# Softmax over the heads of q: the maximum taken off by eight exponentials with a bias, in place of one subtraction on GpSimd

## The chip, the cores and the metric

The kernel runs on one core of a Trainium2 chip. The core has five engines that run their own instruction streams and wait for one another by semaphores: TensorE (PE in the profile, with its weight loads shown apart as PEld), VectorE (DVE), ScalarE (ACT), GpSimd (POOL) and SyncE (SP), which here only starts transfers. The metric is the time of one execution on the device in microseconds (us). Lower is better.

## The reference

Everything is float32. First a linear attention with two softmaxes, then a Fourier mixing layer with a two-layer perceptron:

```
# q, k, v: (batch 8, heads 8, sequence 576, head width 64)
q_s = exp(q - max(q, axis=-1));  q_s = q_s / (sum(q_s, axis=-1) + 1e-9)   # over the 64 of one head
k_s = exp(k - max(k, axis=2));   k_s = k_s / (sum(k_s, axis=2) + 1e-9)    # over the sequence
kv  = einsum('bhsd,bhse->bhde', k_s, v)
x   = einsum('bhsd,bhde->bhse', q_s, kv)          # then laid out as (8, 576, 512)
u   = x + real(fft(fft(x, axis=1), axis=2))
un  = (u - mean(u)) / sqrt(var(u) + 1e-6)
out = u + relu(un @ w_ch1) @ w_ch2                # 512 -> 2048 -> 512
```

The change touches the first line alone: each row of q holds 8 heads of 64 values, and each head has a maximum of its own.

## The kernel before, in words

The eight batch elements are worked through one after the other. For each there is an attention, a Fourier transform with its mixing, a normalisation, and the perceptron. The perceptron does almost all of the multiplying. For the first group of rows it is done plainly (L780 up, L789 down). All later groups use a Strassen scheme (L850 up, L886 down) with seven products in place of eight. Its products gather in the PSUM banks `ba`, `bb`, `bc`; L814 (ScalarE) and L818, L822, L861 (VectorE) take sums of them out, L857 and L862 (ScalarE) are the relus, and L341 to L344 (`a_side`, GpSimd) form the Strassen combinations of the result.

While TensorE does the perceptron of one batch element, the attention of the next one is laid between its steps (`merged`, L1039, L1040). So one stage of the trace, some 122 us long, has an "up" half, in which the attention of the next element runs, and a "down" half, in which its transform, mixing and normalisation run.

The attention of a batch element is a list of items, pipelined over load, exponential, turn (transpose) and product:

- four `k` items (a pair of heads each): `k_exp` takes the maximum (L455), the exponential with the maximum as its bias and the sum as its second output (L457), then `k_turn` (L467, L468, L474, L476) and `k_times_v` (L484, L487);
- four `q` items of 128 tokens by 512 columns (8 heads of 64): `q_exp`, then `q_turn` (four transposes on TensorE, L532; a copy on ScalarE, L539) and `q_times_kv` (L564, copy L566);
- for every second batch element a `t` item, 128 tokens that two elements share: the same `q_exp`, then `t_turn` (L532, L545) and `t_fold`.

That gives 8 x 4 + 4 = 36 runs of `q_exp`. Before the change one run is: maximum over each head on VectorE (L519); subtraction of the eight maxima, spread over 64 columns each, on GpSimd (L520); one exponential over all 512 columns on ScalarE (L521); sum over each head (L523), plus epsilon (L524), reciprocal (L525), product with the reciprocals (L526), all on VectorE. The tiles of q have three buffers (`bufs=3`), the maxima and reciprocals three each.

The order of the instructions on each engine is not written out by hand. The build puts the instructions of each engine into an order of its own from their dependencies and their place in the source, and inserts the waits. In the trace the first exponentials of q for the batch element after the next one stand, for that reason, at the end of an "up" half, ahead of work that comes earlier in the source (L577). Within an engine the order is then fixed: an instruction that waits holds up all behind it.

For the first batch element there is no perceptron to hide behind: its attention, transform and normalisation fill the first 62 us alone, with small matmuls (L206) laid in only to keep TensorE running. Its q lies in the large tile `big`, and one q of the second element lies in `spare`; the other 30 are named `q` in the profile.

## Time and profile before

| | |
|---|---|
| time, median of 3 runs | 1157.17 us (1155.72 to 1157.97) |
| span of the profiled execution | 1153.2 us |
| PE busy | 1102.6 us (96%) |
| DVE busy | 543.1 us (47%) |
| POOL busy | 371.8 us (32%) |
| ACT busy | 352.1 us (31%) |
| mean granted TensorE clock | 0.993 |

Busy time is the sum of the time in which an engine had an instruction in hand. TensorE is busy nearly throughout, so the other engines matter only where TensorE has to wait for them, or where they do before it has begun. The groups of the profile say how often a line ran, how long one took, how long its engine had been idle just before, and what ended that idle time.

The lines of `q_exp` in the trace before: L519 ran 36 times at some 0.68 us, L520 36 times at 1.04 us where nothing else pressed (up to 1.49 us), L521 36 times at 0.63 us, L523 36 times at 0.68 us.

### The profile page before, as it was taken

How to read it: one execution, taken by the hardware profiler on the slowest of the kernel's cores; microseconds unless marked ns; L12 is line 12 of the kernel's file. 1: busy time of each engine (PE TensorE's matmuls, PEld its weight loads, DVE VectorE, ACT ScalarE, POOL GpSimd, SP SyncE). 2: the span in 40 equal slices, each digit the busy share in tenths (PEclk: the TensorE clock that was granted, in tenths of full speed). 3: DMA queues.
4: the chain of work that ended last, by engine and by line, in shares of the span. 5: the costliest groups of instructions: out<-in, count | busy, mean ns of one | idle time of the engine just before them, and what ended most of it. 6: DMA issues, size and time to landing. Idle time of an engine off the chain costs nothing.

```text
span 1153.2 us, 14431 instructions
## 1 busy us (share of the span) xinstructions
PE 1102.6 (96%) x5472; PEld 919.8 (80%) x5472; DVE 543.1 (47%) x1110; ACT 352.1 (31%) x704; POOL 371.8 (32%) x338
## 2 busy tenths in 40 slices
PE   5799989998999999999999999999999999999997
PEld 4644555877888988888889888888889888888886
DVE  6775757368333734376334733583434353202301
ACT  4585422343123412252215222341233142201200
POOL 4075632246103521254023601361033303402320
PEclk9999989999999999999999999999999999999999
DMA  9378765354346534554366334643454344444441
GB/s 313 111 229 267 253 234 191 126 176 158 129 142 202 205 110 150 185 181 147 124 201 212 135 119 149 202 178 137 142 181 153 113 144 167 167 153 153 149 182 55
DMA packets 92548, 193.78 MB, mean 168 GB/s; under 512 B 23088, under 2 KB 59696, under 8 KB 85312
## 3 DMA queue, kind: packets, MB, share of 16 engines
q1 hardware_dynamic: 90680, 191.82, 48.8%
q10 hardware_dynamic: 1800, 1.05, 0.3%
q8 instruction: 43, 0.70, 0.2%
q14 instruction: 25, 0.20, 0.1%
HBM read 168.72 MB, written 28.31 MB: 171 GB/s over the span
## 4 chain that ended last, share of the span: by engine, by line
PE 67%; DVE 7%; ACT 1%; DMA 1%; issue 0%; POOL 0%; POOLq 0%; SPq 0%
PE bb L886 13%; PE bb L850 12%; PE bc L886 10%; PE bc L850 8%; PE ba L850 7%; PE ba L886 7%; PE acc L484 2%; PE acc L564 1%; PE acc L655 1%; PE acc L658 1%; PE tr L750 1%; PE acc L678 1%; DVE eo L603 1%; PE tr L467 1%; PE tr L532 1%; DVE big L861 1%
## 5 line engine op out<-in xcount | busy, mean ns | idle before, releaser
L850 PE MATMUL bb<-unT,big 128*128 128x256 f32 x768 | 187.7, 381 | 2.9 <-DVE u L822 2.8
L886 PE MATMUL bb<-big 128*128 128x256 f32 x768 | 172.8, 379 | 0.0
L850 PEld LDWEIGHTS bb<-unT,big 128*128 128x128 f32 x768 | 142.8, 190 | 26.8 <-DVE u L818 4.1
L886 PEld LDWEIGHTS bb<-big 128*128 128x128 f32 x768 | 145.1, 190 | 20.1
L850 PE MATMUL bc<-unT,big 128*128 128x256 f32 x512 | 125.2, 379 | 0.0
L850 PE MATMUL ba<-unT,big 128*128 128x256 f32 x512 | 124.5, 379 | 0.0
L341 POOL TENSOR_TENSOR big<-big 128x512 f32<-128x512 f32 (+1 forms) x38 | 45.0, 1183 | 246.5 <-ACT big L862 242.0
L886 PE MATMUL bc<-big 128*128 128x256 f32 x512 | 116.5, 379 | 0.5 <-DVE x L903 0.5
L862 ACT ACTIVATE big<-big 128x512 f32<-128x512 f32 x96 | 60.3, 629 | 179.8 <-DVE big L861 179.6
L886 PE MATMUL ba<-big 128*128 128x256 f32 x512 | 114.1, 379 | 0.0
L886 PEld LDWEIGHTS bc<-big 128*128 128x128 f32 x512 | 95.9, 190 | 14.1 <-DVE x L903 0.9
L886 PEld LDWEIGHTS ba<-big 128*128 128x128 f32 x512 | 95.9, 190 | 12.3
L850 PEld LDWEIGHTS bc<-unT,big 128*128 128x128 f32 x512 | 95.5, 190 | 12.5
L850 PEld LDWEIGHTS ba<-unT,big 128*128 128x128 f32 x512 | 95.0, 190 | 11.7
L822 DVE TENSOR_TENSOR u<-bb,s 128x512 f32<-128x512 f32 x40 | 27.6, 690 | 135.7 <-PE bb L886 80.0
L349 POOL TENSOR_TENSOR unT<-unT 128x512 f32<-128x512 f32 x8 | 14.2, 1776 | 174.3 <-DVE unT L348 174.3
L818 DVE TENSOR_TENSOR u<-bb,s 128x512 f32<-128x512 f32 x40 | 27.6, 691 | 82.5 <-PE bb L850 41.7
L898 POOL TENSOR_TENSOR x<-x,u 128x512 f32<-128x512 f32 x14 | 17.8, 1269 | 147.3 <-DVE u L822 118.8
L861 DVE TENSOR_TENSOR big<-bc,u 128x512 f32<-128x512 f32 x64 | 44.0, 688 | 23.1 <-PE bc L850 22.2
L520 POOL TENSOR_TENSOR q<-q,qm 128x512 f32<-128x512 f32 x30 | 32.5, 1089 | 58.1 <-DVE qm L519 22.6
L814 ACT COPY s<-ba 128x512 f32<-128x512 f32 x40 | 23.4, 586 | 91.0 <-PE ba L886 47.5
L342 POOL TENSOR_TENSOR big<-big 128x512 f32<-128x512 f32 (+1 forms) x38 | 47.7, 1254 | 2.0
(224 smaller groups left out, 1652.2 us busy)
## 6 DMA issues: line engine op xcount, KB each, us to landing
big<-w1s SPq DMA_DIRECT2D x64, 896.0 KB
big<-w2s SPq DMA_DIRECT2D x56, 1024.0 KB
big<-in_w_dram SPq DMA_DIRECT2D x21, 512.0 KB
k<-in_kT_dram SPq DMA_DIRECT2D x26, 288.0 KB
q<-in_q_dram SPq DMA_DIRECT2D x27, 256.0 KB
v<-in_v_dram SPq DMA_DIRECT2D x26, 256.0 KB
words<-in_w_dram SPq DMA_DIRECT2D x11, 512.0 KB
w2s<-big SPq DMA_DIRECT2D x8, 512.0 KB
```

The lines of the kernel that those rows point to most:

```text
L341: e1.tensor_tensor(out=to(4), in0=at(2), in1=at(3), op=ALU.add)
L342: e1.tensor_tensor(out=to(2), in0=at(0), in1=at(2), op=ALU.subtract)
L484: nc.tensor.matmul(pk, lhsT=ks[:, c, :], rhs=v[:, c, :], start=(c == 0), stop=(c == NC - 1))
L520: nc.gpsimd.tensor_tensor(out=heads, in0=heads, in1=spread(m), op=ALU.subtract)
L814: nc.scalar.copy(temp("s1"), box["ba"][:])
L818: V.tensor_tensor(out=temp("u2"), in0=box["bb"][:], in1=box["s1"][:], op=ALU.add)
L822: V.tensor_tensor(out=temp("u3"), in0=box["bb"][:], in1=box["s1"][:], op=ALU.add)
L850: nc.tensor.matmul(bank()[:, i, :], lhsT=w[:, WA_AT[m], k * P:(k + 1) * P], rhs=unT[:, B_AT[m], k, :], start=first and i == 0 and k == 0, ...
L861: V.tensor_tensor(out=hp(i), in0=bank[:], in1=u[:], op=ALU.add)
L862: nc.scalar.activation(hp(i), hp(i), ACT.Relu)
L886: nc.tensor.matmul(bank()[:, i, :], lhsT=h[p][:, A_AT[m], i * P:(i + 1) * P], rhs=w[:, p, :], start=first and i == 0 and p == 0, stop=p == ...
L898: nc.gpsimd.tensor_tensor(out=x, in0=x, in1=t[:], op=ALU.add)
```

## The change

The subtraction on GpSimd is left out. The maximum is written with its sign turned, and ScalarE takes it off as the bias of the exponential. A bias is one value per partition, and a row has eight heads with eight maxima, so the one exponential over 512 columns becomes eight over 64 columns. What is computed stays the same. The change takes a step and a hand-over between engines out of the chain, and takes work off GpSimd; ScalarE gets more instructions.

```diff
         m = self.small.tile([P, H], F32, tag="qm", name="qm", bufs=3)
-        V.reduce_max(m[:], heads, axis=AX.X)
-        nc.gpsimd.tensor_tensor(out=heads, in0=heads, in1=spread(m), op=ALU.subtract)
-        nc.scalar.activation(q, q, ACT.Exp)
+        V.reduce_max(m[:], heads, axis=AX.X, negate=True)
+        for h in range(H):
+            nc.scalar.activation(heads[:, h, :], heads[:, h, :], ACT.Exp, bias=m[:, h:h + 1])
         rec = self.small.tile([P, H], F32, tag="qrec", name="qrec", bufs=3)
         V.reduce_sum(rec[:], heads, axis=AX.X)
```

## The prediction

> **What bounds the kernel now.** I read the busy times first, then the granted clock, then who waited for whom on TensorE, then the order of time around the lines that change.

> ```profile
> span 1153.2 us, 14431 instructions
> PE 1102.6 (96%) x5472; PEld 919.8 (80%) x5472; DVE 543.1 (47%) x1110; ACT 352.1 (31%) x704; POOL 371.8 (32%) x338
> L520 POOL TENSOR_TENSOR q<-q,qm 128x512 f32<-128x512 f32 x30 | 32.5, 1089 | 58.1 <-DVE qm L519 22.6
> ```

> TensorE is the bound: it is idle for only 1153.2 - 1102.6 = 50.6 us, of which 62.0 - 38.65 = 23.3 us lie in the first 62 us, where the first batch element is prepared alone (busy times by stretches). Nothing taken off GpSimd or put on ScalarE counts by itself. What counts is what it does to those waits. The list of waits of TensorE names few that touch `q_exp`:

> ```profile
> PE bb L850 <- DVE u L822: 2.8, 1, 2.8
> PE acc L564 <- ACT qT L539: 2.4, 4, 1.7
> PE tr L532 <- DVE big L526: 1.5, 2, 1.0
> PE tr L532 <- DVE q L526: 0.7, 2, 0.4
> PE tr L532 <- DVE qrec L524: 0.5, 1, 0.5
> PE tr L532 <- ACT q L521: 0.3, 1, 0.3
> ```

> (us in all, times, longest.) The largest, 2.8 us, seems to have nothing to do with q. The order of time shows that it has:

> ```profile
> 262.72 0.66 DVE L519 TENSOR_REDUCE qm<-q 128x8 f32<-128x512 f32 x1
> 265.82 1.27 POOL L344 TENSOR_TENSOR big<-big 128x512 f32<-128x512 f32 x1
> 267.05 1.04 POOL L520 TENSOR_TENSOR q<-q,qm 128x512 f32<-128x512 f32 x1
> 268.12 0.63 ACT L521 ACTIVATE q<-q 128x512 f32<-128x512 f32 x1 [4.56 <-POOL q L520]
> 268.79 0.69 DVE L523 TENSOR_REDUCE qrec<-q 128x8 f32<-128x512 f32 x1 [3.33 <-ACT q L521]
> 271.75 0.68 DVE L822 TENSOR_TENSOR u<-bb,s 128x512 f32<-128x512 f32 x1
> 272.48 1.13 PE L850 MATMUL bb<-unT,big 128*128 128x256 f32 x4 [2.85 <-DVE u L822]
> ```

> The maximum was ready at 263.38, but the subtraction stood behind L341 to L344 on GpSimd until 267.05. ScalarE waited for it, VectorE's sum L523 for ScalarE, L822 stood behind that on VectorE, and TensorE waited for L822. So GpSimd's queue did cost TensorE 2.85 us, once. In the later stages (530 us on) TensorE never waits at L532: the exponential is there early.

> [...] L457 (bias, 576 columns) takes 772 ns and L730 (bias, 4 columns) 297 ns, so some 293 fixed with a bias. Four L744, which have two such operands (806 ns each), ran in 2.93 us from 443.76 on: (2.93 - 0.81)/3 = 0.71 us apart, an overlap of 0.10 us.
> [...] L520 took 1.04 us alone, but 1.37 us at 254.60, beside L526 and L861. [...] what negating a maximum costs; L455 does it already, in some 0.75 us for 576 columns, against 0.68 for the 512 of L519, so I cost it at nothing.

> **The change, part by part.**
> Removed: 36 subtractions of 1.04 us, some 37 us of GpSimd, and one hand-over. Nobody waits for the freed GpSimd directly.
> Added: seven more instructions on ScalarE for each of 36 runs. [...] one after another 346 - 96 = 250 ns. Eight: 7 x 0.25 + 0.35 = 2.10 us. No row shows short instructions with a bias in a row. Bounds: L666 follows L664 after only 0.09 us (32 columns, no bias), which would give some 1.1 us; no overlap at all gives 8 x 0.346 = 2.77 us. I take 2.10, since L744 shows the overlap with such operands.
> A lone run of `q_exp`, from the end of the maximum to the end of the exponential. Before: 0.13 (L519 to L520, at 503.05) + 1.04 + 0.03 + 0.63 = 1.83 us. After: 0.04 (L455 to L457, at 491.71) + 2.10 = 2.14 us. So 0.31 us later. ScalarE itself stood still for most of the 1.83 before (it waited for q on GpSimd 25 times, 35.1 us in all), so what stands behind it on ScalarE is late by the same 0.31 us. But where two runs follow each other, GpSimd and ScalarE worked side by side before, one every 1.04 us; now it is one every 2.0 us, so the second is late by 0.31 + 0.96 = 1.27 us. In all ScalarE gets 36 x (2.0 - 0.53) = 53 us more to do, which 31% busy carries.

> What of it reaches TensorE, stretch by stretch, with the order as it is:
> - First element (0 to 62 us, nothing hides anything). Two runs at 15.24 and 15.96 follow each other: the second ends 0.9 us later than 19.15. Behind it on ScalarE stand L545 and L468, and TensorE waits for both already (L474 and L484, at 19.68 and 20.16). The last run (26.26; its subtraction took 1.29 us) loses 0.1 to 0.3. Sum: +1.1.
> - Second element (137 to 163 us). Three runs in a row: 24 short exponentials take 6.1 us, and end at 144.4 in place of 142.9. L468 behind them has 1.25 us to spare; the fourth run gets later on VectorE, and L539 behind it, for which L564 already waits 1.7 us. Sum: +0.8.
> - Third element (240 to 275 us). TensorE waits 0.3 to 0.5 us at four L532, so there is no slack. The first two runs follow each other and VectorE does the second sum ahead of the first product: +1.2; the third adds 0.3. Then the wait at 272.48: the exponential no longer stands behind L344, but all has moved by 1.5 us. Following the same queue, maximum end 264.9, eight exponentials to 267.1, L523 to L526 to 269.0, two L519 to 270.2, L822 to 270.9: TensorE goes on at 270.9 in place of 272.48. Sum of the stretch: -1.6.
> - Stages for elements five and seven (from 498 and 744 us). L539 stands behind two runs on ScalarE and TensorE waits for it already by 0.2 and 0.4 us (507.17, 752.79): each +0.7.
> - Ends of the other "up" halves (388 to 398, 633 to 644 us). Two runs follow each other, VectorE falls back by 0.4 us, and the transform's chain there ends in a TensorE wait of 1.2 us (L655, at 411.73 and 657.17): each +0.4.
> - All other runs: the product L526 ends 2.8 us (505.33 against L532 at 508.17) to 100 us before its transpose. TensorE's L850 hides them.
> Sum: 1.1 + 0.8 - 1.6 + 1.4 + 0.8 = +2.5 us. 1157.2 + 2.5 = 1159.7 us.

> The build orders the instructions anew, since the change gives it other instructions. It can put L545 or L539 between short exponentials, or move transposes. I can't read that from the profile; it is the largest unknown, and I put 3 us on it each way.

> **The rivals.**
> Faster: the queue on GpSimd is what TensorE feels. It costs 2.85 us once and holds ScalarE up 25 times (at most 4.6 us). If the new order hides the longer trains at 16 and 245 us (no +1.1, no +1.5), what stays is the whole 2.85 us and some of the small L532 waits (1.5 us in all): 1157.2 - 4 = 1153 us. Against it: the pairs stand there because their data arrive together.
> No difference: the longer trains lie beside L850 and L886 everywhere but in the first 62 us, and the losses there are paid by the wait at 272. For it: no wait at L532 from 530 us on. 1157 us.
> Much slower: short exponentials with a bias overlap less than L744, 0.35 us each, 2.8 us a run. A run is then 1.0 us later and each of a pair 2.0. The eight or so runs without slack lose some 0.7 us more each, 5.6 us: 1159.7 + 5.6 = 1165 us. Against it: the row of L744.

> **How the numbers follow.** The forecast of 1159.7 has a chance of 0.36, the much slower case 0.11, no difference 0.27, faster 0.26. The bounds of 0.2% are 1154.9 and 1159.5. Slower is the forecast and the much slower case, 0.47; same 0.27; faster 0.26. The range takes in the faster rival and the much slower one, with 2 us more on each side for the order: 1151 to 1167 us.

> **What would show it right or wrong.** L520 is gone and L521 is there 288 times with some 0.35 us each, 0.25 us apart; ACT busy rises by some 36 x (8 x 0.35 - 0.63) = 78 us in the profile's way of counting, POOL falls by 38. The wait of L850 for L822 at 272 us shrinks; the waits of L474, L484 and L532 before 62 us and around 250 us grow. If trains are much longer or shorter than 2.1 us, my price is wrong. If TensorE's idle time of the first 62 us falls, or the waits at 250 us do, the new order has done better than I could read, and the time is below the one before.

## The result, and the profile after

| | before | after |
|---|---|---|
| time, median of 4 runs | 1156.68 us (1155.72 to 1157.97) | 1142.61 us (1140.6 to 1143.67) |
| ratio, 95% interval | | 0.9876 [0.9858, 0.9894] |
| span of the profiled execution | 1153.2 us | 1140.2 us |
| TensorE busy, and not busy | 1102.6, 50.6 us | 1098.6, 41.6 us |

The changed kernel is 14.1 us faster; 1159.7 was predicted, and the time lies below the range. The first lines of the page after, and the group of the new exponentials:

```profile
span 1140.2 us, 14639 instructions
PE 1098.6 (96%) x5472; PEld 919.1 (81%) x5472; DVE 543.4 (48%) x1110; ACT 397.7 (35%) x956; POOL 332.5 (29%) x302
L521 ACT ACTIVATE q<-q,qm 128x64 f32<-128x64 f32 x240 | 61.5, 337 | 10.2 <-DVE qm L519 9.4
```

GpSimd lost 39.3 us of work and ScalarE got 45.6 us more, as the change means it to. The 13.0 us of span are TensorE's: 9.0 us less in which it has nothing in hand, and 4.0 us less for the same 5472 matmuls. The list of TensorE's waits after, the rows of L655, L532, L474, L850 and L564 that answer to those of before (us in all, times, longest):

```profile
PE tr L532 <- DVE q L526: 2.2, 3, 1.3
PE acc L655 <- DVE eo L625: 0.7, 2, 0.6
PE tr L474 <- ACT tq L545: 0.3, 1, 0.3
PE bb L850 <- DVE u L822: 0.3, 1, 0.3
PE acc L564 <- ACT qT L539: 0.2, 1, 0.2
```

Before, these lines had 2.8 for L822, 2.4 for L539, 2.9 for L625, 0.9 for L545, and 3.0 for the four rows of L532 (big, q and qrec from VectorE, q from ScalarE). Four of the five were to grow by the prediction; all four fell, L532 the least (in the third element it did grow, from 1.4 to 2.2).

Where the time went. The first L780, the first L789, and the first L850 or L886 of a stage are the same products in both traces, so the difference of their starts is what had been gained by then (one execution of each kernel; two further profiles of the changed kernel stand beside it below):

| stretch before | what runs beside it | predicted | trace |
|---|---|---|---|
| 0 to 62.6 us | first element alone | +1.1 | -1.6 |
| 62.6 to 120.2 | k of the second element | 0 | -1.4 |
| 120.2 to 208.2 | q of the second element, weights of the Strassen scheme | +0.8 | -4.7 |
| 208.2 to 278.7 | "up" half with the third element | -1.6 | -2.6 |
| 278.7 to the end | the other stages | +2.2 | -2.9 |
| sum | | +2.5 | -13.1 |

**The third element.** All engines after, in the order of time, around the place where L822 stood behind the exponential (rows between are left out):

```profile
255.27 1.27 POOL L344 TENSOR_TENSOR big<-big 128x512 f32<-128x512 f32 x1
257.93 1.26 DVE L519 TENSOR_REDUCE qm<-q 128x8 f32<-128x512 f32 x2
258.83 3.69 ACT L521 ACTIVATE q<-q,qm 128x64 f32<-128x64 f32 x15
261.57 0.68 DVE L822 TENSOR_TENSOR u<-bb,s 128x512 f32<-128x512 f32 x1
262.16 0.68 DVE L523 TENSOR_REDUCE qrec<-q 128x8 f32<-128x512 f32 x1
262.41 1.03 PE L850 MATMUL bb<-unT,big 128*128 128x256 f32 x4
```

ScalarE begins 0.9 us after the first of two maxima has begun; L344 plays no part. L822 now stands ahead of the sum L523 on VectorE, and the L850 behind it starts without a wait.

**The first element.** ScalarE after, where the prediction had the second of two runs 0.9 us late, and with it L545 and L468:

```profile
16.05 2.26 ACT L521 ACTIVATE big<-big,qm 128x64 f32<-128x64 f32 x9 [0.25 <-DVE qm L519]
18.21 0.56 ACT L545 COPY tq<-tr 128x512 f32<-128x512 f32 x1
18.68 0.58 ACT L468 COPY ks<-tr 128x512 f32<-128x512 f32 x1
19.15 2.02 ACT L521 ACTIVATE big<-big,qm 128x64 f32<-128x64 f32 x8
```

The build laid the two copies between the short exponentials (after nine of them), so that they did not wait for the second train. L545, which began at 19.05 before, begins at 18.21, and TensorE's L484 behind them at 19.31 in place of 20.16. The other half of the 1.6 us comes by 31 us: the later runs of q end earlier too, and the two waits of L532 for L526, 1.03 and 0.45 us before, are gone.

**The second element.** ScalarE and TensorE before, at the first product of q with kv:

```profile
148.60 0.63 ACT L521 ACTIVATE spare<-spare 128x512 f32<-128x512 f32 x1 [4.81 <-POOL spare L520]
149.26 0.59 ACT L539 COPY qT<-tr 128x512 f32<-128x512 f32 x1
149.90 0.94 PE L564 MATMUL acc<-kvr,qT 128*128 128x128 f32 x6 [1.70 <-ACT qT L539]
152.26 0.79 PE L564 MATMUL acc<-kvr,qT 128*128 128x128 f32 x2 [1.43 <-DVE kvr L487]
153.70 3.62 PE L789 MATMUL ba<-big 128*128 128x512 f32 x4
```

Both after, at the same place:

```profile
142.33 2.00 ACT L521 ACTIVATE spare<-spare,qm 128x64 f32<-128x64 f32 x8
144.36 0.58 ACT L539 COPY qT<-tr 128x512 f32<-128x512 f32 x1
145.29 0.83 PE L564 MATMUL acc<-kvr,qT 128*128 128x128 f32 x6
147.60 0.49 PE L564 MATMUL acc<-kvr,qT 128*128 128x128 f32 x2 [1.48 <-DVE kvr L487]
148.36 1.88 PE L789 MATMUL ba<-big 128*128 128x512 f32 x4
```

Of two waits one is left, and the four L789 behind them take 1.88 us in place of 3.62: the granted clock was 0.57 on the mean from 151 to 159 us before, and 1.00 in the same window after. The starts of the same products give each its share. Before the first L564 the changed kernel is 2.7 us ahead, at its last product (147.60 against 152.26) 4.7, and at the first L789 behind the halved clock (151.41 against 159.02) 7.6. So the wait brings some 1.9 us of this stretch and the clock some 2.9.

The wait is gone because of the order. On ScalarE, L539 stands behind the exponential of `spare`, whose maximum (L519, VectorE) began at 146.68 before, 9.1 us after the start of the three maxima ahead of it; the build now puts it at 138.73, 3.9 us after their start. The subtraction of `spare` on GpSimd began only 0.17 us after its maximum had ended, so GpSimd's queue held it for almost nothing.

**An "up" half further on.** Rows of GpSimd before, at the end of the stage of the third element, whose "down" half begins at 398.30 before and at 388.16 after:

```profile
394.12 1.37 POOL L520 TENSOR_TENSOR q<-q,qm 128x512 f32<-128x512 f32 x1 [3.25 <-DVE qm L519]
395.45 1.72 POOL L603 TENSOR_TENSOR eo<-x 128x512 f32<-128x512 f32 x1
400.00 1.45 POOL L603 TENSOR_TENSOR eo<-x 128x512 f32<-128x512 f32 x1
```

GpSimd after, at the same place:

```profile
377.96 1.27 POOL L603 TENSOR_TENSOR eo<-x 128x512 f32<-128x512 f32 x1
383.89 1.38 POOL L603 TENSOR_TENSOR eo<-x 128x512 f32<-128x512 f32 x1 [4.67 <-ACT x L566]
```

L603 is the first step of the transform. Its two runs stood behind the subtractions of q for the element after the next, 2.9 us ahead of the "down" half and 1.7 us into it. Without them the build has it 10.2 and 4.3 us ahead. Its chain ended in the wait of L655 for L625 at 411.73, 1.17 us; after, that L655 starts at 400.25 without one. The same happened at 657.17 (1.16 us). It is L603's place that counts, and not the empty queue as such: in a run below that gives GpSimd its old amount of work back, L603 comes 5.0 and 3.7 us ahead of the "down" half, and the wait is gone as well.

### The profile page after: what moved, and what is told of

Its sections match the earlier page's. It is cut to its first block, busy times and chain, and to the rows that moved or that the text cites. A ratio compares the mean times of both kernels' runs of the same rounds, so it can differ in the third digit from the quotient of the medians.

```text
span 1140.2 us, 14639 instructions
## 1 busy us (share of the span) xinstructions
PE 1098.6 (96%) x5472; PEld 919.1 (81%) x5472; DVE 543.4 (48%) x1110; ACT 397.7 (35%) x956; POOL 332.5 (29%) x302
## 4 chain that ended last, share of the span: by engine, by line
PE 79%; DVE 11%; ACT 4%; DMA 2%; issue 2%; POOL 1%; SPq 0%; ACTq 0%; POOLq 0%; DVEq 0%
PE bb L850 14%; PE bb L886 13%; PE bc L886 10%; PE bc L850 9%; PE ba L850 9%; PE ba L886 8%; PE acc L484 3%; PE acc L564 2%; PE bc L789 2%; PE acc L655 2%; PE acc L658 2%; PE acc L678 1%; PE tr L750 1%; PE tr L532 1%; PE tr L467 1%
## 5 line engine op out<-in xcount | busy, mean ns | idle before, releaser
L850 PE MATMUL bb<-unT,big 128*128 128x256 f32 x768 | 187.9, 381 | 0.3 <-DVE u L822 0.3
L886 PE MATMUL bb<-big 128*128 128x256 f32 x768 | 172.8, 379 | 0.0
L850 PEld LDWEIGHTS bb<-unT,big 128*128 128x128 f32 x768 | 142.8, 190 | 23.8 <-DVE u L818 3.4
L886 PEld LDWEIGHTS bb<-big 128*128 128x128 f32 x768 | 145.1, 190 | 20.1
L341 POOL TENSOR_TENSOR big<-big 128x512 f32<-128x512 f32 (+1 forms) x38 | 45.1, 1187 | 309.5 <-ACT big L862 305.6
L850 PE MATMUL bc<-unT,big 128*128 128x256 f32 x512 | 125.3, 379 | 0.0
L850 PE MATMUL ba<-unT,big 128*128 128x256 f32 x512 | 124.3, 379 | 0.0
L886 PE MATMUL bc<-big 128*128 128x256 f32 x512 | 116.5, 379 | 0.5 <-DVE x L903 0.5
L886 PE MATMUL ba<-big 128*128 128x256 f32 x512 | 114.1, 379 | 0.0
L886 PEld LDWEIGHTS bc<-big 128*128 128x128 f32 x512 | 95.9, 190 | 14.1 <-DVE x L903 0.9
L886 PEld LDWEIGHTS ba<-big 128*128 128x128 f32 x512 | 95.9, 190 | 12.3
L850 PEld LDWEIGHTS bc<-unT,big 128*128 128x128 f32 x512 | 95.5, 190 | 12.5
L850 PEld LDWEIGHTS ba<-unT,big 128*128 128x128 f32 x512 | 95.0, 190 | 11.7
L822 DVE TENSOR_TENSOR u<-bb,s 128x512 f32<-128x512 f32 x40 | 27.6, 689 | 134.8 <-PE bb L886 79.1
L521 ACT ACTIVATE q<-q,qm 128x64 f32<-128x64 f32 x240 | 61.5, 337 | 10.2 <-DVE qm L519 9.4
L349 POOL TENSOR_TENSOR unT<-unT 128x512 f32<-128x512 f32 x8 | 14.2, 1773 | 172.9 <-DVE unT L348 172.9
L818 DVE TENSOR_TENSOR u<-bb,s 128x512 f32<-128x512 f32 x40 | 27.6, 690 | 76.8 <-PE bb L850 38.1
L861 DVE TENSOR_TENSOR big<-bc,u 128x512 f32<-128x512 f32 x64 | 44.1, 688 | 26.1 <-PE bc L850 25.3
L754 ACT COPY unT<-tr 128x512 f32<-128x512 f32 x36 | 20.6, 585 | 86.5 <-PE tr L750 86.0
```

The lines of the kernel that those rows point to most:

```text
L341: e1.tensor_tensor(out=to(4), in0=at(2), in1=at(3), op=ALU.add)
L521: nc.scalar.activation(heads[:, h, :], heads[:, h, :], ACT.Exp, bias=m[:, h:h + 1])
L818: V.tensor_tensor(out=temp("u2"), in0=box["bb"][:], in1=box["s1"][:], op=ALU.add)
L822: V.tensor_tensor(out=temp("u3"), in0=box["bb"][:], in1=box["s1"][:], op=ALU.add)
L850: nc.tensor.matmul(bank()[:, i, :], lhsT=w[:, WA_AT[m], k * P:(k + 1) * P], rhs=unT[:, B_AT[m], k, :], start=first and i == 0 and k == 0, ...
L861: V.tensor_tensor(out=hp(i), in0=bank[:], in1=u[:], op=ALU.add)
```

## The experiments

The theory formed from this: **the gain is GpSimd's queue**, of which the subtractions are gone, so that everything behind them on GpSimd, and what follows that on the other engines, comes earlier. Rivals: **the short pieces**, between which the build can lay copies; **ScalarE's and VectorE's shorter chain**, whatever GpSimd does; **the clock**, of which a lucky position of the waits gives or takes a stretch. The short diffs are against the kernel before, where nothing else is said.

### Which part brings it

VectorE subtracts, one exponential, nothing of q on GpSimd:

```diff
-        nc.gpsimd.tensor_tensor(out=heads, in0=heads, in1=spread(m), op=ALU.subtract)
+        V.tensor_tensor(out=heads, in0=heads, in1=spread(m), op=ALU.subtract)
```

> The subtraction goes to VectorE (36 more instructions of some 0.68 us there), the exponential stays one of 512 columns. Theory A (the gain of 14 us comes from taking q out of GpSimd's queue: q stood behind L341 to L344 there, and L603 and L341 stood behind q): most of the gain is here too, 1141 to 1149 us. Theory B (the gain comes from the short exponentials, between which the build can put copies that TensorE waits for): none of it is here, 1154 to 1162 us.

Measured: 1150.52 us, 0.9964 [0.9951, 0.9976]. A part of the gain only, between the two ranges of the expectation. VectorE pays 36 x 0.68 = 24 us for what GpSimd lost. By the first L206 the trace is 1.2 us later than before (the change is 1.6 earlier), TensorE waits 3.1 us for L818 in place of nothing, and L655 waits 3.1 us as before. So with VectorE loaded for it, freeing GpSimd brings about a third of the gain.

The subtraction stays on GpSimd, eight exponentials without a bias:

```diff
-        nc.scalar.activation(q, q, ACT.Exp)
+        for h in range(H):
+            nc.scalar.activation(heads[:, h, :], heads[:, h, :], ACT.Exp)
```

> The subtraction stays on GpSimd, and the exponential is eight of 64 columns without a bias. Theory A: no gain, and the longer trains on ScalarE come on top of the wait for GpSimd, 1156 to 1164 us. Theory B: most of the gain, 1142 to 1149 us.

Measured: 1152.62 us, 0.9971 [0.9959, 0.9983]. It lies in neither range. The first 62 us are 2.1 us longer, the way that the prediction expected of the trains, but in sum the pieces alone bring 0.29%; that the order which they get repays more than they cost is the likely reading, and not shown.

One maximum for the whole row (the 8 heads share it), one exponential with it as the bias, nothing on GpSimd:

```diff
-        V.reduce_max(m[:], heads, axis=AX.X)
-        nc.gpsimd.tensor_tensor(out=heads, in0=heads, in1=spread(m), op=ALU.subtract)
-        nc.scalar.activation(q, q, ACT.Exp)
+        V.reduce_max(m[:, 0:1], q, axis=AX.X, negate=True)
+        nc.scalar.activation(q, q, ACT.Exp, bias=m[:, 0:1])
```

> One maximum over the whole row of 512 columns as the bias of one exponential, in place of one for each head: nothing on GpSimd and no train of short instructions. The softmax over each head stays the same but for rounding, as its maximum cancels; for widely different heads it would be less safe. If the trains of 2.02 us on ScalarE still cost TensorE something (L532 waits 2.2 us for the third element), some 1 to 3 us below the changed kernel. If they are hidden, the same as the changed kernel. Theory B (short pieces help): some us above the changed kernel.

Measured: 1143.57 us, 0.9897 [0.9858, 0.9936], beside 1143.11, 0.9893 [0.9865, 0.992] for the change itself on the same chip (its expectation stands next). One piece of some 0.72 us does as well as eight in 2.02 us. So the short pieces aren't needed for the gain, and in sum they cost nothing here: what both kernels share is that GpSimd has left the chain and VectorE got nothing. The two don't gain in the same places: this one gains 4.5 us in the stretch of the third element, where the changed kernel gains 2.6, and less before it.

> The changed kernel once more, for a second trace and a ratio beside the other runs on the same chip. If the halved clock comes with the waits, its trace has no halved clock between 125 and 165 us again; if it comes by chance, it may have one there and be some 3 us longer. Ratio to before 0.987 to 0.991.

The changed kernel with two useless subtractions on GpSimd behind each maximum (5 x 64 and 3 x 64 columns, the result is not read), so that GpSimd has its old work back while the chain of q doesn't pass through it:

```diff
+        junk = self.work.tile([P, 5, DH], F32, tag="junk", name="junk", bufs=1)
+        for n in (5, 3):
+            wide = m[:, 0:n].unsqueeze(2).to_broadcast([P, n, DH])
+            nc.gpsimd.tensor_tensor(out=junk[:, 0:n, :], in0=wide, in1=wide, op=ALU.subtract)
```

> The changed kernel, with two instructions of 5 and 3 x 64 columns on GpSimd after each maximum, whose output nobody reads (they stand for the time of the subtraction, not for its place in the chain of q). If it is only q's wait in the queue that cost time, the changed kernel's 1143 us stay, within 2 us. If GpSimd's time as such cost it (what stands behind q on GpSimd, and its press on VectorE), part of the gain goes: 1146 to 1154 us. Theory B: no change from 1143 us.

Measured: 1147.84 us, 0.9936 [0.992, 0.9953]. Some 5 to 7 us of the gain are gone (5 by the medians against the changed kernel's, 7 by the ratios). In the trace all of the loss falls in the first three elements (at the first L886, 278.7 us before, only 2.9 us of gain are left, against 10.2); from there to the end it gains 2.4 us, nearly as the change does. In the second element the dummies stand in front of L349 and L341, and TensorE's product waits longer than before the change:

```profile
151.65 0.79 PE L568 MATMUL acc<-kvr,qT 128*128 128x128 f32 x2 [3.88 <-DVE kvr L487]
153.08 3.62 PE L793 MATMUL ba<-big 128*128 128x512 f32 x4
```

(L568 and L793 are L564 and L789; four lines were put in.) So the load on GpSimd costs in the first two elements, and the later ones gain without it being gone. Whether it costs by delaying what stands behind it on GpSimd, by slowing VectorE's operations beside it (last section), or by the order that this kernel got, this run doesn't tell.

### Where it is

The form of after in the first branch, that of before in the second: for the first three elements alone, and for the last five alone (`it[1] >= 3`):

```diff
+        if it[1] < 3:
...
+        else:
...
```

> The changed form for the first three batch elements, the old one for the other five. The marks of the two traces put 10.2 us of 13.1 before the third element's attention ends. Theory A or B with the gain where the traces show it: 1145 to 1149 us. If the later stages with their shorter queues held most of it: 1151 us or more.

> The counterpart of the run with the first three: the changed form for the last five batch elements alone. In the traces the changed kernel gains 2.95 us after the third element's attention, and the run with the first three gained nothing there. If the gain lies where the traces show it, and the stages don't depend on one another: some 3 us below the kernel before, 1151.5 to 1154. If the stages before set the later ones up: no gain.

Measured: 1146.43, 0.9923 [0.9909, 0.9938], and 1148.31, 0.9934 [0.991, 0.9957]. Together these are 0.77% + 0.66% = 1.43%, more than the 1.07% to 1.24% of the whole change in three comparisons: parts don't add up, since each variant gets an order of its own. The second brought more than the expectation had. One cause shows in its trace: the tile behind L344 in the stage of the third element belongs to the element after it, so that "the last five" holds the longest wait, which falls from 2.85 to 1.07 us. Another 3.3 us of its trace lie before 208 us, where its q is that of the kernel before; they are order and clock. The two parts do agree on the ends of the two "up" halves: with the last five changed each gains 1.4 us, with the first three 0.0.

That one tile alone:

```diff
+        if it == ("q", 3, 0, 0):
...
+        else:
...
```

> The changed form for one q tile of 36: the fourth element's first, whose subtraction stood behind L341 to L344 on GpSimd at 263 to 267 us, before TensorE's wait of 2.85 us for L822. If the prediction read that chain right: that wait goes to under 1 us, and the kernel is 2 to 3 us below the one before. If another subtraction or wait takes its place: under 1 us.

Measured: 1151.7 us, 0.9966 [0.9956, 0.9977]; the stretch of the third element is 2.6 us shorter in its trace. Rows of it in the order of time (L522 is the line of the exponentials in this form; with five lines more, L827 and L855 are L822 and L850):

```profile
263.15 2.01 ACT L522 ACTIVATE q<-q,qm 128x64 f32<-128x64 f32 x8
268.88 0.68 DVE L827 TENSOR_TENSOR u<-bb,s 128x512 f32<-128x512 f32 x1
269.62 1.13 PE L855 MATMUL bb<-unT,big 128*128 128x256 f32 x4 [0.29 <-DVE u L827]
```

One run in 36 brings a quarter of the gain, and the wait that the prediction read in the profile, GpSimd's L344 to TensorE, was read rightly: 2.85 us to 0.29.

The one run of `spare` in the second element, which stood on GpSimd ahead of the second wait there:

```diff
+        if it == ("q", 1, 1, 1):
...
+        else:
...
```

> The changed form for one q tile of 36, the one in the spare tile of the second batch element. In the trace before, TensorE waits 1.70 us for L539 behind it, and its clock is at half from 151 to 158 us. If that clock follows from the waits: the wait and some 3 us of clock go, 3 to 5 us below the kernel before. If the clock falls by itself: 1.7 us below at most. If the wait only moves to the next one behind it (L487 for the second product): nothing.

Measured: 1154.31 us, 0.9991 [0.9979, 1.0003]. No difference that can be told. The waits were 1.86 and 0.79 us in place of 1.70 and 1.43, and a halved clock stayed, for 3.41 us in place of 6.83. The maximum of `spare` began at 145.86, 9.1 us after the start of the three maxima ahead of it, as in the kernel before. The second element's gain is not in that one tile, since its place on VectorE didn't move.

### The second element: the clock, or a chain that ends later

The biggest part of the gain, 4.7 us in the profile, has two readings. (In two further profiles of the changed kernel it was 3.1 and 2.7 us; both had a stretch of 3.41 us at half clock from 127 or 128 us on, behind L484.) The two waits of 1.70 and 1.43 us let the clock be halved, and without the first it isn't; or a chain of the other engines ends earlier. To tell them apart, the waits are filled with other work: products of a unit matrix with itself into the same place, ahead of the first and the last product of the first tile, which the real product then overwrites.

```diff
         for r in range(NR):
-            nc.tensor.matmul(px[:, r * P:(r + 1) * P], lhsT=qT[:, r, :], rhs=self.kvr[b % 2][:, r, :], start=True,
-                             stop=True)
+            at = px[:, r * P:(r + 1) * P]
+            for _ in range(12 if it[1:] == (1, 0, 0) and r in (0, NR - 1) else 0):
+                nc.tensor.matmul(at, lhsT=self.ident[:], rhs=self.ident[:], start=True, stop=True)
+            nc.tensor.matmul(at, lhsT=qT[:, r, :], rhs=self.kvr[b % 2][:, r, :], start=True, stop=True)
```

In the kernel before:

> The kernel before, with 24 small matmuls of the unit matrix (128 x 128, some 0.1 us each) laid on TensorE into the two waits of the second element's first product (1.70 us for L539 and 1.43 us for L487 at 148 to 152 us); the product overwrites what they give. They take no time that TensorE doesn't wait anyway. If TensorE's clock falls to half at 151 to 158 us because it has been waiting: no halved clock there, and up to 3 us below the kernel before. If the clock falls whatever TensorE does: the same as the kernel before, or 0.5 us longer.

In the changed kernel, with 24 more ahead of k's first product in that element:

> The same filling on the changed kernel, and 24 small matmuls more ahead of the second element's first product of k with v, where TensorE waits 2.7 to 3.3 us (L484, at 126 us) and the second trace of the changed kernel has a halved clock. If the clock follows from the waits: no halved clock from 120 to 165 us, and 0 to 2 us below the changed kernel (ratio to before 0.986 to 0.989). If not: the changed kernel's time.

Measured: 1165.83 us, 1.0085 [1.007, 1.0099], and 1152.66 us, 0.9974 [0.9964, 0.9984]. Both miss, since the filling was too much: each product shows as two in the trace, and twelve took 2.84 us, more than the wait. In the first there was no halved clock at 150 us, but new waits of 3.33 and 4.44 us at the transform, each with a halved clock behind it; in the second the filling took 5.5 + 2.8 + 2.8 us, which alone is about what it lost against the change, and a halved clock came at 140 us with a new wait of 3.22 us. Neither decides.

Six in place of twelve, in the kernel before (the expectation's "a quarter of an hour's worth less" is a slip for half of the filling of the first):

> The kernel before with 6 + 6 matmuls of the unit matrix in the second element's first product (12 + 12 passes of 0.11 us, some 1.35 us in each of the waits of 1.70 and 1.43 us), a quarter of an hour's worth less than the run before it: the work now fits into the waits. If the clock falls because TensorE waits there: no halved clock from 145 to 165 us in its trace, and 1 to 3 us below the kernel before. If not: the same as the kernel before.

Measured: 1155.69 us, 1.0 [0.999, 1.001]. The filling fits: six take 1.50 us, 0.34 us of the waits are left, and there is no halved clock up to 165 us. That half of the expectation came true: with the waits filled the halved clock goes, and TensorE is ready for the transform's first L655 at 178.2 us, 2.9 us ahead of 181.06 in the kernel before. The gain of time did not come, since TensorE then waits there (L657 and L627 are L655 and L625):

```profile
182.09 0.73 PE L657 MATMUL acc<-ft,eo 128*128 128x144 f32 x4 [3.92 <-DVE eo L627]
```

The chain of waits that ends there, in pieces (start us, us, what; lines up to L392 are those of before):

```profile
139.92 1.23 POOL q L520
145.65 0.68 DVE q L526
146.34 0.33 DVE big L344
149.90 3.87 DMA w1s<-big
154.63 10.40 DMA w2s<-big
165.12 0.44 DVE big L348
167.50 2.98 DMA w2s<-big
170.50 0.43 DVE big L348
```

It runs from GpSimd's subtraction through ScalarE and VectorE to L344, which here forms combinations of the weights (the same helper as on GpSimd) and stands behind the sums and products of q on VectorE. A store (`w1s`) takes these to memory. On SyncE a load that needs it (L392) stands next, and behind that load the stores of other combinations (`w2s`), 10.40 us for the first. L348 overwrites what that store reads, and the transform follows on VectorE.

This chain is not what held the kernel before. There the second L625, which L655 waits for, had ended 2.9 us before L655 began:

```profile
177.87 0.48 DVE L625 TENSOR_TENSOR eo<-eo 128x128 f32<-128x128 f32 x2
181.06 0.66 PE L655 MATMUL acc<-ft,eo 128*128 128x144 f32 x4
```

(the row holds two runs, of which the first ended at 178.16). In the filled kernel it ended at 181.95. Its build put a maximum of k and a third L348, which waits for a second store of 2.98 us, ahead of VectorE's L603: that starts at 173.13 there and at 167.22 before. So the filling took away the clock's loss, and an order of its own gave it back.

In the changed kernel the same chain comes early. VectorE before, at the L348 behind the first store:

```profile
164.70 0.43 DVE L348 TENSOR_TENSOR big<-big 128x256 f32<-128x256 f32 x1 [11.43 <-DMA w2s<-big]
```

VectorE after:

```profile
158.25 0.43 DVE L348 TENSOR_TENSOR big<-big 128x256 f32<-128x256 f32 x1 [9.74 <-DMA w2s<-big]
```

It comes 6.4 us earlier, of which 3.0 had been gained by 120 us, and L625 ends at 171.97, 1.5 us before L655 at 173.45. Had it gained only those 3.0 us, L655 would have waited some 1.7 us (an estimate: 178.16 - 3.0 against 173.45). So the earlier chain was needed for a part of the 4.7 us.

### A version beyond both

Since TensorE still waits three times (2.2 us) at L532 in the third element, that element's exponential was made in one piece again, behind a subtraction on VectorE; the others as changed (a diff against the changed kernel, which ran beside it):

```diff
+        if it[1] == 2:
+            V.reduce_max(m[:], heads, axis=AX.X)
+            V.tensor_tensor(out=heads, in0=heads, in1=spread(m), op=ALU.subtract)
+            nc.scalar.activation(q, q, ACT.Exp)
+        else:
...
```

> The changed form, but for the third batch element the subtraction on VectorE and one exponential of 512 columns (as in the run with the subtraction on VectorE, which gained 4.0 us in that stretch, where the changed kernel gained 2.6 and waits 2.2 us at L532). If the trains on ScalarE cost that, those waits go and it is 1 to 2 us below the changed kernel. If VectorE's 0.68 us a run cost as much: the same.

> The changed kernel beside the run with VectorE for the third element, on the same chip. Ratio to before 0.987 to 0.991.

Measured: 1141.94 us, 0.9874 [0.9861, 0.9887], and 1142.27, 0.9878 [0.9864, 0.9891]: no difference. The waits of L532 for L526 are gone, but others came in their place: 0.7 us for L857, 1.1 in two for L539, 0.3 each for L818 and L822 (by the names of after). No version was found that is faster than the change.

## Why the prediction was wrong

**Right.** The price of the train: 2.10 us worked out, 2.02 measured, pieces of 337 ns on the mean (346 worked out) that follow each other by 0.24 us. The rows of the trace before give its terms: L457 and L730, both with a bias, took 772 ns for 576 columns and 297 for 4, which is 0.83 ns a column and some 294 for the rest, so some 347 for 64 columns (an estimate from these two); and the four L744 of 806 ns in 2.93 us overlap by 0.10 us each. GpSimd's work, 38 to fall and 39.3 fallen. ScalarE's rise, 78 in the profile's way of counting, was 45.6, since overlapping pieces count once (240 of 337 ns make 80.9 us, and the page has 61.5); nothing in the time hung on that. The third element: L344's hold on TensorE, -1.6 net, was -2.6, and the run with that one tile shows the wait go. The sign that it gave for a time below the one before, less idle time in the first 62 us, came true.

**Wrong, and it is what decided: "Nobody waits for the freed GpSimd directly", and with it the whole list worked out "with the order as it is".** The order was no disturbance of 3 us each way around a sum; it was most of the effect. Four terms failed by it:

- First element, +1.1 predicted, -1.6 in the trace. The pair of trains did not stand as a block in front of L545 and L468; the build laid these between, and the last runs of q, which were to lose 0.1 to 0.3 us, no longer held L532.
- Second element, +0.8 predicted, -4.7, -3.1 and -2.7 in three profiles. The prediction had L539 later, behind longer trains; it came 4.9 us earlier, 2.2 of these gained here, since the build moved the maximum of `spare` ahead. Nor did it look at the granted clock around the waits that it named: of the 4.7 us the wait of 1.70 us makes some 1.9, and the halved clock behind it some 2.9. It also stopped at L564 and did not ask what stood behind q on VectorE, the chain through the stores, which had to come earlier too.
- Ends of two "up" halves, +0.8 predicted, and with the waits of 1.17 and 1.16 us gone, -1.4 each. The prediction had seen those waits, and the subtractions in front of L603 on the same page, but put L655's wait down to VectorE, where the releaser's name stands, and not to the place of L603 on GpSimd ahead of it.
- Elements five and seven, +1.4 predicted; their waits for L539 are gone too.

The remaining -1.4 us, between 62 and 120 us, is a stretch of halved clock which in the kernel before lay on the L780 products (5.4 us for what takes 3.6), and in the changed one on the small L206 that only keep TensorE running. That place is in part chance: of the six traces whose first two elements, but for `spare` or the filling, are those of the kernel before, three have a halved clock at the first L780 and three have not; of the three of the changed kernel none has.

The rival "faster" named GpSimd's queue, which is the mechanism in the third element, but counted only its one visible wait and some waits of L532: 4 us. More of the size would have come from asking, at each of TensorE's waits, what stood in front of the whole chain and not only in front of the engine that released it, and from reading the clock behind it.

**What stays open.** GpSimd's queue itself is shown as the cause in the third element alone, by the run with one tile (2.6 us in its trace, 0.34% of the time). The share of the clock in the whole can only be estimated: its mean was 0.991 over 91 runs of the kernel before and 0.996 over 12 of the changed one, which over 1150 us is some 5 us of the 13 or 14, or three stretches of 3.41 us at half rate. Why the build moves the maximum of `spare`, L603 and L545 as it does was not varied. How much of the whole is the free GpSimd, and how much is an order that happens to suit: a part of the change can't be made with the order of all else held fast, and the experiments that held back some of it (0.9964, 0.9971, 0.9936, 0.9923, 0.9934) don't add up. That the maximum over the whole row, with another set of instructions, gives the same time speaks for GpSimd's place in the chain and against luck, but it is one case, and it gains in other places.

## What to carry to other kernels

When an operation leaves an engine with an in-order queue, follow what stood behind it there, and behind its followers on their engines, through to stores and reused buffers, up to the engine that sets the end; a wait need not be due to the engine that the list names last. A forecast "with the order as it is" says little where a build reorders everything: an engine at 32% of busy time can hold up the one at 96% at places that don't show its name. Behind each wait look at the granted clock, and ask for the next limit before calling a wait free: where one is filled, another can end last.

## What was not expected of the hardware

**The halved clock, behind waits of 2.15 us and more, and in a grid.** In the sixteen traces, after the first 70 us, every wait of TensorE of 3.2 us or more (ten of them, 3.22 to 4.44 us) was followed by a stretch at half clock. So were six of 2.15 to 2.98 us, while ten others of 2.18 to 2.94 us were not (the 2.85 us up to 272.48 before is one of them); and the 1.70 + 1.43 us within 4.4 us in the kernel before were followed by one.

```profile
148.08:151.49 3.41, 1.05 (x7) 0.74 (x6) 3.41 (x10) 1.22 (x2) 0.49 (x1) 1.00 0.57 231
145.49:148.90 3.41, 1.93 (x14) 1.50 (x13) 2.90 (x8) 0.72 (x2) 1.08 (x2) 1.00 1.02 351
```

That is 2.36 us idle before, and 1.48 after. At a granted clock of 0.50 a stretch of 3.41 us costs 1.7 us, and one of 6.83 us 3.4 (estimates, half of each); in the three of 6.83 us TensorE was idle again for 0.74 us or more within the first half (0.77 before). Where the grid lies differs from trace to trace (62.74 before and 49.92 after are 3.76 windows apart), and waits of much the same length came with and without a halved clock: the changed kernel waited 2.69, 3.32 and 2.92 us at L484 in its three profiles, with at most 1.62, 3.16 and 2.22 us of that in one window, and without, with and with a halved clock.

**VectorE beside GpSimd.** An operation of VectorE with two inputs of 512 columns, L526, took 0.68 us in the changed kernel with GpSimd idle, and 1.59 us beside L342 and L343:

```profile
140.44 0.68 DVE L526 TENSOR_TENSOR q<-q,qrec 128x512 f32<-128x512 f32 x1
252.47 1.59 DVE L526 TENSOR_TENSOR q<-q,qrec 128x512 f32<-128x512 f32 x1
```

In the kernel with the dummy operations L349 and L341 fell on this line, and it took 1.21 us at 142.50 and 146.76. VectorE's busy time as a whole stayed (543.1 us before, 543.4 after), so that this moved single instructions and not the sum.
